# Weighted sums of attention issued once per head instead of twice, with a reordered start and double conversion buffers, in a fused attention and MLP kernel

## The chip, the cores and the metric

The kernel runs on one core of one Trainium2 chip. The metric is the device time of one execution in microseconds, as the median of several runs. The engines are TensorE (PE, with its weight loads as PEld), VectorE (DVE), ScalarE (ACT), GpSimd (POOL) and SyncE (SP, which here only issues DMAs).

## What is computed

Inputs are `q`, `k`, `v` of 2 batches, 8 heads, 768 positions and 64 features. The reference, cut to what matters:

```python
q_bits = (np.einsum('bhsd,dk->bhsk', q, proj) > 0)     # 6 bits each
mask = q_bucket[:, :, :, None] == k_bucket[:, :, None, :]
scores = np.where(mask, scale * q @ k.T, -1e9)
attn = exp(scores - max); attn = attn / (sum + 1e-9)
x = (attn @ v) with heads side by side                 # [2, 768, 512]
h = relu(x @ w_in); u, v = halves of h
v_s = w_spatial @ layernorm(v) + b_spatial
x = (u * v_s) @ w_out                                  # the first MLP, "moe1"
out = x + relu(layernorm(x) * g_ln @ w_ch1) @ w_ch2    # the second MLP
```

The weights of the MLPs arrive as 64-bit floats.

## The kernel before, in words

**A planner sets the order.** The body doesn't issue instructions. Each call on `nc` goes to `Plan.add`, which makes a job of it, notes which earlier jobs it must follow, and gives it a cost from a table (`Plan.cost`). Consecutive PE calls of the same shape into the same PSUM tile become one job that isn't broken up: up to 6 calls, or 12 where an fp32 matmul is less than 256 columns wide. `settle` lays all jobs out over time several times, with a latest due time for each job, and `issue` writes out the best order it found, engine by engine. So the order of every engine's queue comes from these costs and due times, and a changed cost or job moves instructions far away as well. All instructions are issued from one line of `issue`, line 492; the profile's rows are therefore told apart by tile names.

**Parts.** Part 0 is the attention of both batches, with `moe1` of batch 0 mixed into the attention of batch 1. Part 1 is `moe1` of batch 1 together with the begin of the second MLP; part 2 is the rest of the second MLP. An engine finishes its jobs of a part before it takes those of the next.

**Attention.** It goes through 96 query tiles of 128 queries: for each batch, for each of 8 heads, two groups (`g`) of three tiles (`j`). `attn_step` handles one tile:

- `scores`: four PE matmuls fill `sc` (128 x 768, two PSUM buffers of pool `ps_s`) from `qs` and `ks`. For each of two column ranges, one pass takes all 128 rows and a second takes 76 rows, of which 12 are mask rows, which make the score of a masked-out pair very large.
- `masked_max`: DVE reads `sc`, writes `x` to SBUF and its row extremes `nb`.
- `exps`: ACT takes exponentials of `x` in place, and sums them.
- `transposes`: six PE transposes turn `x` through PSUM tiles `pt` (two of 384 columns, pool `ps_b`, four buffers); ACT or DVE copies each to `e`, the transposed exponentials of a whole group (128 x 6 x 384, `EB` = 2 buffers).
- `weighted`: after a group's last tile, the product with `v`. `vv` is the stationary operand, 128 x 64, and `e` the moving one. Each group makes 12 calls: for each of the six key tiles, the left half of PE's columns takes the first 192 queries of the group and the right half the other 192. The sums `po` are in PSUM, 64 partitions for each half, and ACT copies one half to `xT`, DVE the other. An fp32 matmul shows as two records in the trace, so a group has 24 records of 128 x 192.
- `summed` and `normalized`: for each pair of heads, the sums' reciprocals are made (`zr`, `zw`), transposed through `pz`, and multiplied into `xT`.

`passes_of` moves high parts, low parts and mask rows into `ks` and `qs` by DMA from SP's queue, for each head and each query group.

**The start.** For head pair 0 the raw `k` and `q` are loaded (`pair_load`), and rows 64 to 127 of head 0's operands come by a second load, `dup` (`first_load`, in a buffer of `e`). `mismatch` makes the mask: PE multiplies raw `k` and `q` with `sides` (the projection `pj` with its signs, 32 columns for each of four quarters) into `pm` of 128 x 384, and DVE turns that into `m`. `first_parts` makes the operands of head 0 directly, without DMAs: high parts, low parts (`ks`, `qs`) and copies of the mask rows from `m`. `pair_split` makes the high parts (ACT) and low parts (DVE) of the whole pair, from which DMAs fill the operands of the second query group and of head 1. Before and after stand some PE transposes without use of their result (`warm`).

**Conversions.** While attention runs, 12 pieces of the first MLP's weights are converted: a 512 KB load on ACT's DMA queue into `f64`, `words_f64` with one ACT and five DVE instructions that use a second tile `f64c`, `join_f64` on POOL, and a split into high and low parts on ACT and POOL. Pool `conv0` has `CB0` = 1 buffer for each of the two tiles.

The change touches `Plan.__init__`, `Plan.add` and `Plan.cost`, the constants `CB0` and `EB`, the loads of `pj`, `mismatch`, `weighted`, `attn_step` and the calls that open part 0.

Of the kernel before, what the change touches and what calls it, by code (L numbers as in the profile page):

```python
# [18 lines left out]
P = 128  # L19
# [150 lines left out]
class Plan:  # L170
# [14 lines left out]
    RATE = {"load": 300e3, "move": 195e3, "store": 200e3}  # L185

    def __init__(self, tc):
        self.tc, self.jobs, self.pools, self.part = tc, [], [], 0
        for name, key in (("tensor", "PE"), ("vector", "DVE"), ("scalar", "ACT"), ("gpsimd", "POOL"), ("sync", "SP")):
            setattr(self, name, Engine(self, key))  # L190

    def add(self, engine, op, args, kw):
        writes = [kw["out"] if "out" in kw else args[0]]
        rest = [*(args if "out" in kw else args[1:]), *(x for k, x in kw.items() if k not in ("out", "accum_out"))]
        if "accum_out" in kw:
            writes.append(kw["accum_out"])
        reads = [x for x in rest if isinstance(x, View)]
        views = [(x, True) for x in writes if isinstance(x, View)] + [(x, False) for x in reads]
        prev = self.jobs[-1] if self.jobs else None
        if (  # L200
            engine == "PE"
            and prev is not None
            and prev.engine == "PE"
            and prev.part == self.part
            and not prev.closed
            and prev.out is writes[0].base
            and prev.kind == (op, cells(writes[0]), writes[0].rows)
            and len(prev.calls) < (12 if cells(writes[0]) < 256 and op == "matmul" and reads[0].dtype == F32 else self.RUN)
        ):
            job = prev  # L210
        else:
            job = Job(len(self.jobs), engine, self.part)
            self.jobs.append(job)
            if engine == "PE":
                job.out, job.kind = writes[0].base, (op, cells(writes[0]), writes[0].rows)
        busy, lag = self.cost(engine, op, writes, [x for x in rest if hasattr(x, "dtype")], kw, job)
        job.calls.append((op, args, kw))
        job.busy, job.lag = job.busy + busy, lag
        for x, w in views:
            for j, box, w2 in x.base.uses:  # L220
                if (w or w2) and j is not job and all(a < d and c < b for (a, b), (c, d) in zip(box, x.place)):
                    job.after.add(j)
            x.base.uses.append((job, x.place, w))
        return None
# [5 lines left out]
    def cost(self, engine, op, writes, reads, kw, job):  # L230

        out = writes[0]
        n = cells(out)
        if op == "dma_start":
            src = kw["in_"]
            sbuf = lambda x: isinstance(x, View) and not x.base.ring.pool.dram
            job.way = "store" if not sbuf(out) else "move" if sbuf(src) else "load"
            job.bytes = 4 * n * (out.rows if isinstance(out, View) else src.rows if isinstance(src, View) else 128)
            if engine == "ACT":
                return 0.4, 0.0  # L240
            return (0.84 if n <= 512 and job.bytes < 32768 else 0.61 if job.bytes < 200000 else 0.45), 0.0
        psum = any(isinstance(x, View) and x.base.ring.pool.psum for x in (out, *reads))
        if engine == "PE":
            if op == "transpose":
                return (0.109 if isinstance(reads[0], View) else 0.213), 0.165
            if reads[0].dtype == F32:
                return n * (0.00083 if out.rows == 64 else 0.00042) + 0.006 + (0 if job.calls else 0.2), 0.2
            return n * 0.4375e-3 + 0.0065, 0.17
        if engine == "ACT":
            if "accum_out" in kw:  # L250
                return 0.93, 0.1
            return 0.05 + n * 0.9e-3, 0.1
        if engine == "DVE":
            one = len([x for x in reads if cells(x) > 8]) < 2
            if op == "bn_stats":
                return 0.59, 0.1
            if n < 32:
                job.shared = not psum and op == "tensor_scalar"
                return 0.08, 0.11
            fast = op == "tensor_scalar" and one and not psum and "accum_out" not in kw  # L260
            job.shared = not psum and op in ("tensor_scalar", "scalar_tensor_tensor")
            held = sum(1 for x in reads if cells(x) == 1)
            return 0.065 + n * (0.53e-3 if fast else 1.04e-3) + 0.06 * held, 0.085
        if op == "memset":
            return 0.145, 0.05
        if kw.get("op") == ALU.pow:
            return 0.45 + 0.25 * n, 0.05
        return (0.06 + n * 2.42e-3 if op == "tensor_tensor" else 0.19 + n * 0.84e-3), 0.03
# [229 lines left out]
def attn_moe_kernel(ctx: ExitStack, tc: tile.TileContext, qT, kT, v, proj, w_in, w_spT, b_sp, w_out, g_ln, w1, w2, out):  # L498
# [14 lines left out]
    NKT = S // P  # L513
    GRP = 3
    TB = 4
    CB0 = 1
    VB = (((0, 1, 2), (3, 4, 5)), ((0, 1), (2, 3, 4), (5,)))
    CB = 2
    CONV_AT = (5, 9, 14, 19, 24, 29, 34, 39, 44, 49, 53, 57)
# [11 lines left out]
    AT = (-10, -7, -6, -4, 0)  # L531
    PO = 2
    KCUT = (0, 2)
    EB = 2
    GW = GRP * P
    NG = NQT // GRP
    KC = S // 2
# [57 lines left out]
    NM = 2 * NB  # L595
    MR = D + NM
    pj = const.tile([P, NB], F32, name="pj")
    for a in range(2):
        nc.scalar.dma_start(out=pj[a * D : (a + 1) * D], in_=proj)


    HROW = 3 * NB
# [95 lines left out]
    def mismatch(b, r):  # L698
# [9 lines left out]
            )  # L708
        nc.vector.tensor_scalar(m, pm, above, worth, op0=ALU.is_gt, op1=ALU.mult)
        pairs[b, r]["m"] = m  # L710

    order = [(b, h, g, j) for b in range(B) for h in range(H) for g in range(NG) for j in range(GRP)]
    NT = len(order)
# [119 lines left out]
            else:  # L833
                nc.vector.tensor_copy(e, pt)

    def weighted(b, h, g):
        gm = f"{b}_{h}_{g}"
        gr = groups[b, h, g]
        po = ps_b.tile([P, 512], F32, tag="b", name=f"po_{gm}")

        HW = GW // 2
        for kt in range(NKT):
            for a in range(2):
                nc.tensor.matmul(
                    po[a * D : (a + 1) * D, :HW],
                    heads[b, h]["vv"][:, kt],
                    gr["e"][:, kt, a * HW : (a + 1) * HW],
                    start=(kt == 0),
                    stop=(kt == NKT - 1),
                )  # L850
        groups.pop((b, h, g))
        own = slice(h % 2 * D, (h % 2 + 1) * D)
        at = g * GW
        nc.scalar.activation(xT[b][own, h // 2, at : at + HW], po[0:D, :HW], AF.Copy)
        nc.vector.tensor_copy(xT[b][own, h // 2, at + HW : at + GW], po[D:P, :HW])

    def summed(b, r):

# [18 lines left out]
    def attn_step(i):  # L877
# [9 lines left out]
        if 0 <= i + 1 < NT:  # L887
            masked_max(*order[i + 1])
            exps(*order[i + 1])
        if 0 <= i - PO < NT and order[i - PO][3] == GRP - 1:  # L890
            weighted(*order[i - PO][:3])
        for late, e in ((1, summed), (3, normalized)):
            n = i - PO - late
            if 0 <= n < NT and order[n][1] % 2 == 1 and order[n][2:] == (NG - 1, GRP - 1):
# [241 lines left out]
            nc.tensor.transpose(warm, ident, ident)  # L1136
    pair_load(0, 0, first=True)
    dup = first_load()
    mismatch(0, 0)
    first_parts(dup)  # L1140
    pair_split(0, 0, first=True)
    for _ in range(WARM2):
        nc.tensor.transpose(warm, ident, ident)
    head_prep3(0, 0)
# [220 lines left out]
```

## Time and profile before

| | us |
|---|---|
| runs: median of 3 | 674.24 |
| runs: lowest and highest | 673.82, 676.37 |
| profiled execution, device time | 673.77 |
| profiled execution, span of its instructions | 671.5 |
| PE covered by matmul records | 656.8 (98%) |
| PEld | 535.3 (80%) |
| DVE | 436.6 (65%) |
| ACT | 304.7 (45%) |
| POOL | 195.9 (29%) |

The times of rows are microseconds from the start of the span, which is 2.3 us shorter than the execution's device time. An engine's busy time is the union of its records. The end of a matmul record is modelled, and matmuls overlap, so PE's steps are read from the starts of records, not from their lengths. "Idle before" in a row is the time in which the engine had nothing to do just before, with the engine or DMA that ended it.

### The profile page before, as it was taken

The numbers are of one execution on the slowest core, as the hardware profiler recorded it, in microseconds if no ns is written. First come the engines' busy times: TensorE is split into PE (matmuls) and PEld (weight loads), VectorE is DVE, ScalarE is ACT, GpSimd is POOL, SyncE is SP. The second block draws the span as 40 slices with busy tenths as digits, with TensorE's granted clock in tenths as the row PEclk, the third lists the DMA queues.
The fourth block names the chain that finished last, engine by engine and source line by source line (L and its number), as shares of the span: only waits on it lengthen the run. The fifth ranks groups of instructions, "written<-read, shape, count | busy, mean of one in ns | idle before, by whom it ended". The sixth has DMA issues, their size and how long they took to land.

```text
span 671.5 us, 10197 instructions
## 1 busy us (share of the span) xinstructions
PE 656.8 (98%) x3760; PEld 535.3 (80%) x3760; DVE 436.6 (65%) x820; ACT 304.7 (45%) x597; POOL 195.9 (29%) x184
## 2 busy tenths in 40 slices
PE   7999999999999999999999999999999999999997
PEld 6887777877788788887778888888888888888886
DVE  5889778897666554444699697766893258962122
ACT  4887777876565644443364344432331122321110
POOL 2333324344341431110224424134442014540000
PEclk7999999999999999999999999999999999999999
DMA  6676766747536824452652441632220022310031
GB/s 180 163 180 164 199 155 145 195 114 190 187 68 210 246 64 131 159 193 95 227 179 91 146 143 62 215 118 86 85 94 1 15 79 86 102 33 0 1 126 62
DMA packets 47417, 83.78 MB, mean 125 GB/s; under 512 B 5676, under 2 KB 32136, under 8 KB 46344
## 3 DMA queue, kind: packets, MB, share of 16 engines
q1 hardware_dynamic: 34024, 53.64, 28.5%
q10 hardware_dynamic: 13344, 29.50, 13.6%
q8 instruction: 30, 0.49, 0.3%
q14 instruction: 19, 0.16, 0.1%
HBM read 51.42 MB, written 12.58 MB: 95 GB/s over the span
## 4 chain that ended last, share of the span: by engine, by line
PE 77%; DVE 9%; DMA 7%; ACT 3%; issue 3%; POOL 1%; SPq 1%; ACTq 0%; DVEq 0%; POOLq 0%
PE pc L492 20%; PE acc L492 20%; PE pg L492 8%; PE sc L492 6%; PE po L492 6%; PE pv L492 5%; PE pt L492 5%; PE py L492 4%; DMA f_v<-in_w_in 3%; DVE x L492 2%; DMA f_w<-in_w 1%; ACT x L492 1%; DVE f64c_v L492 1%; PE ptr_g L492 1%; DMA f_u<-in_w_in 1%
## 5 line engine op out<-in xcount | busy, mean ns | idle before, releaser
L492 PE MATMUL pc<-xh,w1t 128*128 128x512 f32 x576 | 142.0, 394 | 0.0
L492 PE MATMUL acc<-w2t,ch 128*128 128x512 f32 x576 | 141.2, 393 | 0.0
L492 PEld LDWEIGHTS acc<-w2t,ch 128*128 128x128 f32 x576 | 108.1, 188 | 24.6
L492 PEld LDWEIGHTS pc<-xh,w1t 128*128 128x128 f32 x576 | 108.0, 188 | 24.6
L492 ACT ACTIVATE x<-x,nb 128x768 f32<-128x768 f32 x96 | 89.7, 935 | 36.6 <-DVE x L492 32.9
L492 DVE TENSOR_SCALAR_CACHE_REDUCE x<-sc 128x768 f32<-128x768 f32 x96 | 90.7, 953 | 20.3 <-PE sc L492 11.9
L492 PE MATMUL sc<-ks,qs 128*128 128x512 f32 (+3 forms) x384 | 94.4, 368 | 6.2 <-DVE qs L492 3.3
L492 DVE SCALAR_TENSOR_TENSOR ch<-pc,ch 128x512 fp32r<-128x512 f32 x48 | 33.0, 687 | 87.9 <-ACT ch L492 87.7
L492 ACT ACTIVATE ch<-pc 128x512 fp32r<-128x512 f32 x48 | 28.6, 596 | 127.3 <-PE pc L492 127.0
L492 PE MATMUL pt<-ident,x 128*128 128x128 f32 x576 | 82.4, 276 | 1.3 <-ACT x L492 0.6
L492 PEld LDWEIGHTS sc<-ks,qs 128*128 128x128 f32 (+1 forms) x384 | 64.8, 194 | 21.4 <-issue 7.2
L492 POOL TENSOR_TENSOR f64c_w<-f_w,f64c_w 128x512 f32<-128x512 f32 x32 | 44.7, 1398 | 123.3 <-DVE f64c_w L492 108.0
L492 PEld LDWEIGHTS pt<-ident,x 128*128 128x128 f32 x576 | 66.7, 141 | 13.3 <-ACT x L492 3.3
L492 PE MATMUL po<-e,vv 128*64 128x192 f32 x768 | 69.5, 330 | 1.1 <-DVE xT L492 1.0
L492 ACT ACTIVATE e<-pt 128x384 f32<-128x384 f32 x120 | 55.5, 485 | 31.8 <-PE pt L492 31.1
L492 PEld LDWEIGHTS po<-e,vv 128*64 128x64 f32 x768 | 52.4, 137 | 12.5 <-issue 2.4
L492 DVE COPY e<-pt 128x384 f32<-128x384 f32 x72 | 39.6, 553 | 21.6 <-PE pt L492 21.0
L492 DVE TENSOR_SCALAR f64c_w<-f64c_w 128x512 f32<-128x512 f32 (+1 forms) x64 | 38.7, 607 | 19.1 <-ACT f64c_w L492 18.3
L492 PE MATMUL pg<-vn,w_sp 128*128 128x512 f32 x180 | 45.1, 400 | 0.0
L492 ACT ACTIVATE f64c_w<-f_w 128x512 f32<-128x512 f32 x32 | 21.4, 669 | 46.5 <-DMA f_w<-in_w 43.9
L492 PEld LDWEIGHTS pg<-vn,w_sp 128*128 128x128 f32 x180 | 33.0, 188 | 7.8 <-issue 0.6
L492 PE MATMUL pv<-w_v,act_x 128*128 128x512 f32 x144 | 36.4, 398 | 0.6 <-DVE act_x L492 0.6
(132 smaller groups left out, 790.7 us busy)
## 6 DMA issues: line engine op xcount, KB each, us to landing
f_w<-in_w ACTq DMA_DIRECT2D x32, 512.0 KB
ks<-k SPq DMA_DIRECT2D x45, 192.0 KB
qs<-q SPq DMA_DIRECT2D x31, 192.0 KB
wst_sp<-in_w_spT SPq DMA_DIRECT2D x12, 384.0 KB
w_out<-ws_out SPq DMA_DIRECT2D x2, 2048.0 KB
vv<-in_v SPq DMA_DIRECT2D x16, 192.0 KB
ot<-y_dram SPq DMA_DIRECT2D x12, 256.0 KB
qs<-q SPq DMA_DIRECT2D x31, 96.0 KB
```

Source lines behind the costliest of these rows:

```text
L492: getattr(getattr(nc, engine[j.engine]), op)(*map(live, args), **{k: live(x) for k, x in kw.items()})
```

## The change

- `weighted` is called once per head, after both of its groups. There are again 12 calls, but the left half of PE's columns takes all 384 queries of group 0, the right half those of group 1. The copies to `xT` are one of 384 columns on ACT and one on DVE per head.
- `e` has three buffers instead of two.
- The planner keeps the 12 calls of 384 fp32 columns as one job, and counts 0.27 us instead of 0.2 for the first call of an fp32 job.
- Everything that `pair_split` of the first pair issues, high parts and low parts, now waits for the mask `m` (`plan.behind`).
- One of the two loads of `pj` is issued by SP instead of ACT.
- `conv0` has two buffers each of `f64` and `f64c`.

```diff
--- before.py
+++ after.py
@@ -185,7 +185,7 @@
     RATE = {"load": 300e3, "move": 195e3, "store": 200e3}
 
     def __init__(self, tc):
-        self.tc, self.jobs, self.pools, self.part = tc, [], [], 0
+        self.tc, self.jobs, self.pools, self.part, self.behind = tc, [], [], 0, None
         for name, key in (("tensor", "PE"), ("vector", "DVE"), ("scalar", "ACT"), ("gpsimd", "POOL"), ("sync", "SP")):
             setattr(self, name, Engine(self, key))
 
@@ -205,7 +205,7 @@
             and not prev.closed
             and prev.out is writes[0].base
             and prev.kind == (op, cells(writes[0]), writes[0].rows)
-            and len(prev.calls) < (12 if cells(writes[0]) < 256 and op == "matmul" and reads[0].dtype == F32 else self.RUN)
+            and len(prev.calls) < (12 if cells(writes[0]) == 384 and op == "matmul" and reads[0].dtype == F32 else self.RUN)
         ):
             job = prev
         else:
@@ -213,6 +213,8 @@
             self.jobs.append(job)
             if engine == "PE":
                 job.out, job.kind = writes[0].base, (op, cells(writes[0]), writes[0].rows)
+        if self.behind:
+            job.after.add(self.behind)
         busy, lag = self.cost(engine, op, writes, [x for x in rest if hasattr(x, "dtype")], kw, job)
         job.calls.append((op, args, kw))
         job.busy, job.lag = job.busy + busy, lag
@@ -244,7 +246,7 @@
             if op == "transpose":
                 return (0.109 if isinstance(reads[0], View) else 0.213), 0.165
             if reads[0].dtype == F32:
-                return n * (0.00083 if out.rows == 64 else 0.00042) + 0.006 + (0 if job.calls else 0.2), 0.2
+                return n * (0.00083 if out.rows == 64 else 0.00042) + 0.006 + (0 if job.calls else 0.27), 0.2
             return n * 0.4375e-3 + 0.0065, 0.17
         if engine == "ACT":
             if "accum_out" in kw:
@@ -513,7 +515,7 @@
     NKT = S // P
     GRP = 3
     TB = 4
-    CB0 = 1
+    CB0 = 2
     VB = (((0, 1, 2), (3, 4, 5)), ((0, 1), (2, 3, 4), (5,)))
     CB = 2
     CONV_AT = (5, 9, 14, 19, 24, 29, 34, 39, 44, 49, 53, 57)
@@ -531,7 +533,7 @@
     AT = (-10, -7, -6, -4, 0)
     PO = 2
     KCUT = (0, 2)
-    EB = 2
+    EB = 3
     GW = GRP * P
     NG = NQT // GRP
     KC = S // 2
@@ -595,8 +597,8 @@
     NM = 2 * NB
     MR = D + NM
     pj = const.tile([P, NB], F32, name="pj")
-    for a in range(2):
-        nc.scalar.dma_start(out=pj[a * D : (a + 1) * D], in_=proj)
+    nc.sync.dma_start(out=pj[0:D], in_=proj)
+    nc.scalar.dma_start(out=pj[D:P], in_=proj)
 
 
     HROW = 3 * NB
@@ -708,6 +710,7 @@
             )
         nc.vector.tensor_scalar(m, pm, above, worth, op0=ALU.is_gt, op1=ALU.mult)
         pairs[b, r]["m"] = m
+        return plan.jobs[-1]
 
     order = [(b, h, g, j) for b in range(B) for h in range(H) for g in range(NG) for j in range(GRP)]
     NT = len(order)
@@ -833,26 +836,22 @@
             else:
                 nc.vector.tensor_copy(e, pt)
 
-    def weighted(b, h, g):
-        gm = f"{b}_{h}_{g}"
-        gr = groups[b, h, g]
-        po = ps_b.tile([P, 512], F32, tag="b", name=f"po_{gm}")
-
-        HW = GW // 2
+    def weighted(b, h):
+        po = ps_b.tile([P, GW], F32, tag="b", name=f"po_{b}_{h}")
         for kt in range(NKT):
-            for a in range(2):
+            for g in range(NG):
                 nc.tensor.matmul(
-                    po[a * D : (a + 1) * D, :HW],
+                    po[g * D : (g + 1) * D],
                     heads[b, h]["vv"][:, kt],
-                    gr["e"][:, kt, a * HW : (a + 1) * HW],
+                    groups[b, h, g]["e"][:, kt],
                     start=(kt == 0),
                     stop=(kt == NKT - 1),
                 )
-        groups.pop((b, h, g))
         own = slice(h % 2 * D, (h % 2 + 1) * D)
-        at = g * GW
-        nc.scalar.activation(xT[b][own, h // 2, at : at + HW], po[0:D, :HW], AF.Copy)
-        nc.vector.tensor_copy(xT[b][own, h // 2, at + HW : at + GW], po[D:P, :HW])
+        nc.scalar.activation(xT[b][own, h // 2, 0:GW], po[0:D], AF.Copy)
+        nc.vector.tensor_copy(xT[b][own, h // 2, GW:S], po[D:P])
+        for g in range(NG):
+            groups.pop((b, h, g))
 
     def summed(b, r):
 
@@ -887,8 +886,8 @@
         if 0 <= i + 1 < NT:
             masked_max(*order[i + 1])
             exps(*order[i + 1])
-        if 0 <= i - PO < NT and order[i - PO][3] == GRP - 1:
-            weighted(*order[i - PO][:3])
+        if 0 <= i - PO < NT and order[i - PO][2:] == (NG - 1, GRP - 1):
+            weighted(*order[i - PO][:2])
         for late, e in ((1, summed), (3, normalized)):
             n = i - PO - late
             if 0 <= n < NT and order[n][1] % 2 == 1 and order[n][2:] == (NG - 1, GRP - 1):
@@ -1136,9 +1135,11 @@
             nc.tensor.transpose(warm, ident, ident)
     pair_load(0, 0, first=True)
     dup = first_load()
-    mismatch(0, 0)
+    made = mismatch(0, 0)
     first_parts(dup)
+    plan.behind = made
     pair_split(0, 0, first=True)
+    plan.behind = None
     for _ in range(WARM2):
         nc.tensor.transpose(warm, ident, ident)
     head_prep3(0, 0)
```

## Rows read from the trace of the kernel before

**Rows 1.** Windows: span, length, busy us of PE, PEld, DVE, ACT, POOL, clock, DMA.

```profile
24.00:136.00 112.00, 109.36 (x904) 88.54 (x902) 95.14 (x200) 88.02 (x196) 43.41 (x41) 1.00 0.68 169
150.00:317.00 167.00, 165.07 (x1095) 135.61 (x1096) 93.28 (x201) 86.15 (x176) 45.78 (x42) 1.00 0.51 152
317.00:671.00 354.00, 349.88 (x1551) 284.23 (x1549) 220.67 (x365) 105.77 (x179) 96.24 (x70) 1.00 0.29 94
```

**Rows 2.** Waits of PE in the whole run: us in total, times, longest.

```profile
PE sc L492 <- DVE qs L492: 3.3, 1, 3.3
PE sc L492 <- DMA qs<-q: 0.8, 1, 0.8
PE sc L492 <- DVE f64c_out L492: 0.6, 1, 0.6
```

**Rows 3.** Timeline of PE around the first block, short windows: start, length.

```profile
22.36 0.82 PE L492 MATMUL pt<-ident,x 128*128 128x128 f32 x6
...
23.11 0.55 PE L492 MATMUL po<-e,vv 128*64 128x192 f32 x4
...
24.78 0.49 PE L492 MATMUL po<-e,vv 128*64 128x192 f32 x4
25.21 0.33 PE L492 MATMUL pt<-ident,x 128*128 128x128 f32 x1
```

**Rows 4.** Timeline of PE around one mask.

```profile
26.01 0.52 PE L492 MATMUL pm<-k,sides 128*32 128x384 f32 x2
...
26.36 0.49 PE L492 MATMUL pm<-k,sides 128*32 128x384 f32 x2
```

**Rows 5.** Groups of the whole run: count, busy us, mean ns, idle before.

```profile
L492 PEld LDWEIGHTS po<-e,vv 128*64 128x64 f32 x768 | 52.4, 137 | 12.5 <-issue 2.4 <-DVE xT L492 1.2 <-ACT e L492 1.2
L492 ACT ACTIVATE xT<-po 64x192 f32<-64x192 f32 x32 | 10.2, 320 | 10.1 <-PE po L492 7.8 <-DVE xT L492 2.0
L492 DVE COPY xT<-po 64x192 f32<-64x192 f32 x32 | 11.5, 359 | 23.8 <-ACT xT L492 18.8 <-PE po L492 4.5
L492 ACT ACTIVATE e<-pt 128x384 f32<-128x384 f32 x120 | 55.5, 485 | 31.8 <-PE pt L492 31.1
L492 DVE COPY e<-pt 128x384 f32<-128x384 f32 x72 | 39.6, 553 | 21.6 <-PE pt L492 21.0
```

**Rows 6.** Timeline of the start, all engines: start, length.

```profile
5.83 0.32 DVE L492 TENSOR_SCALAR sides<-pj 64x6 f32<-64x6 f32 x3 [1.35 <-DMA pj<-in_proj]
...
6.88 0.95 POOL L492 TENSOR_SCALAR ks<-dup 64x768 fp32r<-64x768 f32 x1 [3.44 <-DMA dup<-in_kT]
...
6.99 0.49 PE L492 MATMUL pm<-q_raw,sides 128*32 128x384 f32 x2
7.05 1.58 DVE L492 SCALAR_TENSOR_TENSOR k<-k_raw,k 128x768 fp32r<-128x768 f32 x1
8.56 0.94 DVE L492 SCALAR_TENSOR_TENSOR q<-q_raw,q 128x768 fp32r<-128x768 f32 x1
...
9.42 0.66 DVE L492 TENSOR_SCALAR m<-pm,above,worth 128x384 fp32r<-128x384 f32 x1
...
10.42 0.88 SPq L492 DMA_DIRECT2D qs<-m  x1
...
10.82 4.64 PE L492 MATMUL sc<-ks,qs 128*128 128x512 f32 x12 [3.33 <-DVE qs L492]
...
16.39 1.09 PE L492 MATMUL sc<-ks,qs 128*128 128x512 f32 x4
```

**Rows 7.** Windows of the start, columns as in rows 1.

```profile
7.50:9.80 2.30, 0.00 (x0) 0.00 (x0) 2.30 (x3) 0.31 (x1) 0.33 (x1) 1.00 0.70 178
9.90:16.60 6.70, 5.78 (x19) 4.80 (x20) 4.34 (x10) 3.01 (x7) 1.10 (x2) 0.50 0.61 165
16.70:20.00 3.30, 3.30 (x25) 2.97 (x24) 2.49 (x5) 2.80 (x7) 0.46 (x1) 1.00 0.82 253
```

**Rows 8.** Groups from 24 to 136 us: count, busy us, mean ns.

```profile
L492 DVE TENSOR_SCALAR_CACHE_REDUCE x<-sc 128x768 f32<-128x768 f32 x47 | 44.3, 950 | 7.3 <-PE pt L492 3.0 <-PE sc L492 2.9 <-ACT e L492 0.9
```

## The prediction

> **What bounds the kernel now.** I read the windows first, to see which engine fills which stretch. TensorE (PE) is covered for 349.88 of 354 us after the attention and for 165.07 of 167 us in the second batch, so there the end is set by PE's own work [rows 1]. In the first batch, 24 to 136 us, PE is covered for 109.36 of 112 us, but VectorE (DVE) is busy for 95.14 us and ScalarE (ACT) for 88.02: two engines run close behind it. Next the waits of PE, which are few: the longest, 3.3 us, is at the very start, a scores matmul that waits for DVE's `qs` [rows 2]. So a microsecond taken out of PE's queue, or off its start, is a microsecond of the end, provided that DVE and ACT keep up in the first batch. The parts are costed in that order.
>
> **Part 1, the weighted sums.** Today 32 blocks of 24 PE records each. One is seen in [rows 3]: it starts at 23.11, and the next instruction starts at 25.21, so a block holds PE for 2.10 us. The records come in pairs, one for each column half. In the last four records (0.49 us, one record lasting 0.33) the second pair starts 0.16 us after the first; in the first four (0.55 us) it starts 0.22 after. The last pair starts at 24.94 and the next instruction at 25.21, 0.27 later. So the block is 0.22, ten steps of 0.162, and 0.26: twelve steps of 0.162 and some 0.16 us that every block pays at its two ends. The entry costs more: the last of six transposes starts at 22.91 (five steps of 0.11 after 22.36), and the block 0.20 after it, where another transpose would start after 0.11: 0.09.
>
> After the change there are 16 blocks, again of 24 records, each over 384 columns. Twice the step is 0.324; twelve of them and 0.16 are 4.05 us. Per head: two blocks with two entries, 4.38, against 4.05 and 0.09, 4.14: 0.24 less, times 16 heads **3.8 us** off PE. No row shows this matmul. The nearest with 384 columns is the mask's, whose second pass starts 0.35 us after its first, at 26.01 and 26.36 [rows 4]. Twelve steps of that plus the 0.10 at the exit are 4.30, 4.39 with the entry, and nothing is gained; that is the lower bound. If the 0.002 over 0.16 belongs to a record and not to a column, and the end cost shrinks to 0.10, it is 0.32 a step, 3.94 a block, 5.6 us in all: the upper bound. I stay near the doubled step, because the 0.35 is the first step of its block, and first steps are longer here too (0.22 against 0.16).
>
> A block covers the load of its weights today: a weight load lasts 137 ns [rows 5] and a pair has two of them, yet a pair takes 0.162 us. The Trainium skill, "TensorE: Matmul & The Clock Gate", under "The mechanism" of packing, says that loads overlap running matmuls only where the row group differs, and the two halves here have the same rows. By that rule the loads would be exposed and halving them would give far more; the step of 0.162 us speaks against it.
>
> The copies out of PSUM also halve in number: ACT 32 of 320 ns become 16 of about 485 (its copy of 384 columns), DVE 32 of 359 become 16 of about 553 [rows 5]. That is 10.2 to 7.8 us and 11.5 to 8.8 us. I count nothing for it: both lie beside PE. It helps part 4.
>
> **Part 2, the start.** The mask's matmuls end at 7.48, but DVE makes the mask `m` only at 9.42, since it does the low parts of `k` (7.05, 1.58 us) and of `q` (8.56, 0.94 us) first [rows 6]. After `m` come the low part of `qs` and the mask rows' copies, and 1.4 us after the start of `m` the first scores, at 10.82. Put straight behind the matmuls, `m` starts near 7.55: 1.9 us earlier, and the scores near 8.9. Next late would be POOL's copy of `dup`, done at 7.83, which is early enough. What moves behind: DVE's 2.52 us, and the two high parts on ACT, which has little to do before the first exponentials (3.01 of 6.7 us from 9.9 to 16.6). What now waits for `m` on ACT and DVE has behind it in their queues the first exponentials and maxima, which need scores that need `m` themselves, so no one is held up who could run; POOL has no part in it. DVE's 2.52 us must fit in the gaps between the first row maxima: in those 6.7 us DVE is busy for 4.34 [rows 7], so most fits; I charge 0.4. Their DMAs move too: `qs<-m`, the last of SP's transfers for query group 1, was issued at 10.42, and the first tile to use it has its scores at 16.39. Two microseconds later for it and two earlier for the scores leave some 2 us; SP issues it behind the low part of `q`, and behind it stand the transfers for head 1, needed much later. One `proj` load goes from ACT's queue to SP's: DVE waited for the second until 5.83, the last 1.35 us of it idle, so `sides` can come sooner; but if SP takes it first, the raw loads each shift by one issue (0.88 us for `qs<-m`). I count these as zero, plus or minus 0.9. Net **1.5 us** gained; bounds: 1.5 lost (all 2.52 and the 0.9 come back against 1.9) and 3.3 gained (the whole wait).
>
> **Part 3, the second conversion buffer.** PE's only wait on a conversion is 0.6 us (`f64c_out`), and its only wait on a DMA is 0.8 [rows 2]. Larger reach for the 512 KB loads could take the first away or lengthen the second. Zero, between 0.6 gained and 0.8 lost.
>
> **Part 4, the coarser block.** Sixteen blocks of 2.10 us fill PE in the first batch; the rest of its 109.36 us is 75.8 for 47 tiles, 1.61 us a tile. DVE needs 95.14 / 47 = 2.02 a tile [rows 1, 8]. So between blocks DVE is the slower one, and it catches up while PE is in a block. Two score buffers let it do two maxima of 0.95 us: 1.9, nearly a block of today. In a block of 4.05 it has 2.15 us beyond them, for which it needs other work: a copy of `e` (0.55), one of `xT`, or a conversion's words. Where it finds only the copy of `e`, it idles 1.6 us a head. Its slack is (112 - 95.14) / 8, 2.1 us a head, so most is absorbed; I charge 0.2 a head for eight heads, 1.6. The second batch, with DVE at 93.28 of 167 us, pays nothing. Bounds: 0.5 gained by the shorter copies, 12.8 lost (8 x 1.6).
>
> **The sum** for this execution (span 671.5, time 673.77; the median of the runs, 674.24, is 0.47 above it): -3.8 - 1.5 + 0 + 1.6 = -3.7, so 670.1; for a median I say 670.2.
>
> **Rivals.**
> A, the start goes better than costed. The granted clock was still 1.00 up to 9.8 us and 0.50 (1.2 GHz) from 9.9 to 16.6, after PE had stood idle from 7.5 to 10.8 [rows 7]. If scores from 8.9 on keep it up, the first three tiles take 1.09 us each, as the four records at 16.39 do, and not 4.64 / 3 = 1.55 [rows 6]: 1.4 us more. With 0.7, half of the 1.35, from `proj` coming early: 668.0. Against it, ACT was the busiest engine right after, 2.80 of 3.30 us at full clock.
> B, slower: DVE runs dry in the long block and PE waits for it between blocks. Place: the first batch, every head; price: 1.6 us times 8, so 673.8 - 5.3 + 12.8 = 681.3. It decides when DVE's idle time in a block exceeds its slack, which needs DVE to have no conversion at hand there. For it: 85% busy. Against: conversions are spread over the batch.
> C, a block isn't cheaper (0.35 a step): 673.8 - 1.5 + 1.6 = 673.9, no change. For it, the only row with 384 columns; the change would then not do what it says.
> D, the low parts return in full at the start, 2.1 us more than charged, so the order gains nothing: 672.2.
> E, the loads are exposed as the page has it: half of 52.4 us of weight loads goes [rows 5], 673.8 - 26.2 = 647.6. The pair step speaks against it.
>
> **How the numbers follow.** Forecast 50 (40 of it below the bound), A 13, B 10, C 14, D 11, E 2. A measurement here tells about 0.5%, 3.4 us, from no change: faster below 670.9. Faster: 40 + 13 + 2 = 55; same: 10 + 14 + 11 = 35; slower: B, 10. The range leaves out B, E and the edges of A: 665.5 to 675.0.
>
> **What would show it.** Right: 384 `po` records of 128x384 in 16 blocks, each some 4.0 to 4.1 us from its first start to the next instruction, their busy total near 66 us against 69.5; first scores near 9 us with `m` before the low parts; PE's cover in the first batch still near 98%. Wrong: a block of 4.3 us (C), scores still after 10 us or a new wait on `qs` for the fourth tile (D), PE idle for over 1 us a head after a block with DVE `x` as releaser (B), or a clock that never falls at the start (A).

## The result, and the profile after

The changed kernel takes **669.14 us** (median of 7 runs, 665.71 to 672.32), the kernel before 674.24 (7 runs, 673.48 to 676.37): ratio 0.9912, interval 0.9884 to 0.994. It is faster by some 5 us; 670.2 was forecast. The profiled execution took 669.14, its span 666.8 us. In the changed kernel all instructions come from line 494.

The windows of the changed kernel answer to [rows 1], with the same columns:

```profile
24.00:136.00 112.00, 109.50 (x740) 78.21 (x742) 97.68 (x200) 89.94 (x196) 43.38 (x41) 1.00 0.71 184
150.00:317.00 167.00, 166.66 (x943) 127.47 (x942) 92.75 (x192) 83.81 (x167) 46.32 (x41) 1.00 0.51 162
317.00:667.00 350.00, 343.95 (x1521) 279.87 (x1519) 211.71 (x358) 103.53 (x173) 96.95 (x70) 1.00 0.26 87
```

PE is covered in the first batch as it was (109.50 of 112 us; cover alone doesn't tell how far PE got), with DVE busier (97.68 against 95.14). In the last stretch 6 us are uncovered, where 4.1 were before. PE's waits in the whole run (us in total, times, longest), which answer to [rows 2]:

```profile
PE sc L494 <- DVE x L494: 3.6, 3, 1.7
PE pv L494 <- ACT xT L494: 2.2, 1, 2.2
PE sc L494 <- DVE qs L494: 1.8, 2, 1.5
...
PE sc L494 <- DMA qs<-m: 0.7, 1, 0.7
```

The wait on `qs` at the start shrank from 3.3 to 1.5 us at most. Longer are the waits of scores on the row maxima (`x`; before there was one, of 0.5 us), the longest at the start, and new is one of 2.2 us on ACT's copy `xT`, in the first MLP of batch 1.

**A block.** PE's timeline around the first block (start, length), short windows as in [rows 3]:

```profile
27.56 0.27 PE L494 MATMUL pt<-ident,x 128*128 128x128 f32 x1
27.76 0.87 PE L494 MATMUL po<-e,vv 128*64 128x384 f32 x4
...
31.04 0.81 PE L494 MATMUL po<-e,vv 128*64 128x384 f32 x4
31.36 0.49 PE L494 MATMUL po<-e,vv 128*64 128x384 f32 x2
31.78 0.50 PE L494 MATMUL sc<-ks,qs 128*128 128x512 f32 x1
```

The block starts at 27.76 and the next instruction at 31.78: 4.02 us. Pairs follow each other after 0.32 (31.04, 31.36), the last pair holds PE for 0.42, and the entry after a transpose takes 0.20 as before. All 16 blocks measure 4.02. Their groups (count, busy us, mean ns, idle before), against [rows 5]:

```profile
L494 PE MATMUL po<-e,vv 128*64 128x384 f32 x384 | 65.5, 490 | 0.0
L494 DVE COPY xT<-po 64x384 f32<-64x384 f32 x16 | 9.0, 560 | 29.3 <-ACT xT L494 24.7 <-PE po L494 4.5
L494 ACT ACTIVATE xT<-po 64x384 f32<-64x384 f32 x16 | 7.7, 484 | 23.1 <-PE po L494 22.5 <-DVE xT L494 0.4
```

**The start**, timeline of DVE and PE, against [rows 6]:

```profile
7.55 0.68 DVE L494 TENSOR_SCALAR m<-pm,above,worth 128x384 fp32r<-128x384 f32 x1 [1.94 <-PE pm L494]
...
8.96 0.47 PE L494 MATMUL sc<-ks,qs 128*128 128x512 f32 x1 [1.52 <-DVE qs L494]
...
9.60 1.47 DVE L494 SCALAR_TENSOR_TENSOR q<-q_raw,q 128x768 fp32r<-128x768 f32 x1
...
10.99 0.95 DVE L494 SCALAR_TENSOR_TENSOR k<-k_raw,k 128x768 fp32r<-128x768 f32 x1
11.86 0.94 DVE L494 TENSOR_SCALAR_CACHE_REDUCE x<-sc 128x768 f32<-128x768 f32 x1
...
12.86 1.65 PE L494 MATMUL sc<-ks,qs 128*128 128x512 f32 x4 [1.74 <-DVE x L494]
```

The mask comes at 7.55 and the first scores at 8.96. But `q`'s and `k`'s low parts now stand between the first scores and their maximum, which starts at 11.86; before, it started at 12.79:

```profile
12.79 0.96 DVE L492 TENSOR_SCALAR_CACHE_REDUCE x<-sc 128x768 f32<-128x768 f32 x1 [1.37 <-PE sc L492]
```

Of 1.9 us, 0.9 is left at that point, and nothing at the sixth maximum, which starts at 20.84 (before at 20.53). The windows of the start, columns as above:

```profile
9.00:12.00 3.00, 1.85 (x8) 1.23 (x8) 2.96 (x5) 1.14 (x2) 1.04 (x1) 1.00 0.24 51
12.00:16.00 4.00, 3.14 (x11) 2.88 (x12) 2.82 (x7) 2.78 (x6) 0.00 (x0) 0.51 0.94 203
16.00:20.00 4.00, 4.00 (x20) 3.65 (x19) 1.88 (x4) 2.74 (x7) 0.00 (x0) 0.64 0.81 219
```

DVE is full from 9 to 12 (2.96 of 3 us), and the granted clock still falls to its lower level, only later than in [rows 7]. It also rises later, at about 18.9 us (an estimate from the mean of 0.64, as 0.50 up to there and 1.00 after), where it was up again by 16.7; part of what was lost up to the sixth maximum may be that.

**Where 2 us went back.** PE began the first MLP of batch 1, the begin of part 1, at 317.10 before and at 310.41 after. These are the first matmuls behind that border, the kernel before first:

```profile
317.10 0.70 PE L492 MATMUL pv<-w_v,act_x 128*128 128x512 f32 x2
...
310.41 0.73 PE L494 MATMUL pv<-w_v,act_x 128*128 128x512 f32 x2
```

PE was 6.7 us ahead there; at the end of the span 4.7 were left. The timeline of the changed kernel behind the border, where ACT loads and converts pieces of the second MLP's weights:

```profile
325.03 1.90 POOL L494 TENSOR_TENSOR f64c_w<-f_w,f64c_w 128x512 f32<-128x512 f32 x1 [3.80 <-DVE f64c_w L494]
...
326.95 0.39 ACTq L494 DMA_DIRECT2D f_w<-in_w  x1
...
327.44 0.60 ACT L494 ACTIVATE xT<-pv 128x512 f32<-128x512 f32 x1 [4.00 <-POOL f64c_w L494]
...
328.09 1.75 PE L494 MATMUL pv<-w_u,act_x 128*128 128x512 f32 x6 [2.18 <-ACT xT L494]
```

ACT issues the third load of these pieces at 326.95, just after POOL has joined the first piece and so freed a buffer. The copy `xT` stands behind that issue in ACT's order and starts after 4.00 us of idle time, and PE waits 2.18 us for it. Then the clock falls:

```profile
325.00:330.00 5.00, 2.82 (x11) 1.95 (x11) 4.82 (x11) 2.37 (x4) 4.14 (x3) 0.95 0.33 106
330.00:334.00 4.00, 4.00 (x13) 3.15 (x12) 2.06 (x5) 1.56 (x3) 0.51 (x1) 0.64 0.00 1
```

At a mean granted clock of 0.64 for 4 us, PE does 2.6 us of full-clock work, so the spell costs about 1.4 us more by this estimate.

### The profile page after: what moved, and what is told of

The parts are those of the page before. It is cut to its first block, busy times and chain, and to the rows that moved or that the text cites. A ratio compares the mean times of both kernels' runs of the same rounds, so it can differ in the third digit from the quotient of the medians.

```text
span 666.8 us, 9374 instructions
## 1 busy us (share of the span) xinstructions
PE 651.5 (98%) x3376; PEld 510.2 (77%) x3376; DVE 430.3 (65%) x804; ACT 302.1 (45%) x581; POOL 198.3 (30%) x184
## 4 chain that ended last, share of the span: by engine, by line
PE 87%; DVE 7%; DMA 3%; issue 1%; ACT 1%; POOL 0%; SPq 0%; ACTq 0%; DVEq 0%; POOLq 0%
PE pc L494 20%; PE acc L494 20%; PE pv L494 8%; PE po L494 8%; PE sc L494 8%; PE pg L494 8%; PE pt L494 7%; PE py L494 5%; DVE x L494 2%; DMA f_w<-in_w 1%; DVE f64c_u L494 1%; PE pm L494 1%; PE ptr_g L494 1%; PE px_c L494 1%; DMA qs<-m 1%
## 5 line engine op out<-in xcount | busy, mean ns | idle before, releaser
L494 PE MATMUL po<-e,vv 128*64 128x384 f32 x384 | 65.5, 490 | 0.0
L494 PEld LDWEIGHTS po<-e,vv 128*64 128x64 f32 x384 | 26.2, 137 | 31.3 <-issue 30.1
L494 PE MATMUL pv<-w_u,act_x 128*128 128x512 f32 x144 | 36.3, 400 | 2.3 <-ACT xT L494 2.2
L494 DVE TENSOR_SCALAR f64c_w<-f64c_w 128x512 f32<-128x512 f32 x64 | 32.6, 511 | 7.2 <-ACT f64c_w L494 6.5
```

Source lines behind the costliest of these rows:

```text
L494: getattr(getattr(nc, engine[j.engine]), op)(*map(live, args), **{k: live(x) for k, x in kw.items()})
```

## The experiments

Runs of one set share a chip and the runs of the kernel before. Times are medians.

| set | kernel | us (lowest to highest) | ratio to before (interval) |
|---|---|---|---|
| 1 | sums_only | 669.25 (668.41 to 671.18) | 0.9920 (0.9899 to 0.9942) |
| 1 | start_only | 673.99 (671.53 to 675.60) | 0.9991 (0.9977 to 1.0005) |
| 1 | buffers_only | 669.47 (669.07 to 671.18) | 0.9925 (0.9904 to 0.9946) |
| 1 | split_columns | 665.82 (664.85 to 667.25) | 0.9867 (0.9847 to 0.9888) |
| 2 | after_again | 668.80 (665.60 to 670.77) | 0.9923 (0.9899 to 0.9946) |
| 2 | cost_only | 672.59 (670.73 to 677.12) | 0.9986 (0.9965 to 1.0006) |
| 2 | buffers_same_order | 671.05 (670.33 to 673.74) | 0.9964 (0.9951 to 0.9977) |
| 2 | late_load | 665.41 (664.62 to 666.38) | 0.9881 (0.9857 to 0.9904) |
| 3 | old_start | 663.74 (662.84 to 666.54) | 0.9843 (0.9819 to 0.9867) |
| 3 | late_low | 665.07 (663.30 to 668.74) | 0.9862 (0.9833 to 0.9891) |
| 3 | fill_start | 665.31 (663.47 to 666.69) | 0.9853 (0.9829 to 0.9877) |
| 3 | late_low_fill | 664.11 (662.59 to 670.02) | 0.9848 (0.9817 to 0.9879) |

The kernel before: 674.43, 674.24 and 674.31 in the three sets.

### Each part alone: sums_only, start_only, buffers_only

Each is the kernel before with one part of the change; the planner then makes a new order. sums_only has `weighted` per head, the third buffer of `e`, the job of 12 calls and the cost of 0.27:

```diff
-    EB = 2
+    EB = 3
...
-    def weighted(b, h, g):
+    def weighted(b, h):
...
```

> The kernel before with the weighted sums once per head and the third buffer of e alone; the start and the conversion buffers stay. Theory: what the change gives is the fixed cost at the ends of 16 blocks that are gone. So 16 blocks of 4.02 us, PE records of po covering 65.5 us against 69.5, and 668.5 to 671.5 us, 3 to 5 below before. Rival (the start or the buffers carry the gain): 672.5 to 675 us.

Measured 669.25: 5.2 us faster, and `po` is busy for 65.5 us as in the changed kernel. start_only has the mask first and one load of `pj` on SP:

```diff
+    nc.sync.dma_start(out=pj[0:D], in_=proj)
...
+    plan.behind = made
     pair_split(0, 0, first=True)
+    plan.behind = None
```

> The kernel before with the new start alone (mask ahead of the low parts, one load of proj on the sync queue). Theory: first scores near 9.0 us and not 10.8, but the two low parts then stand ahead of the first row maximum, so the third tile's scores wait for DVE and most of the 1.9 us is given back: 672.5 to 674.5 us. Rival (the start carries the gain): 669 to 671.5 us.

Measured 673.99, an interval that holds no change. buffers_only:

```diff
-    CB0 = 1
+    CB0 = 2
```

> The kernel before with two conversion buffers alone. Theory: no term of the sum, 672.5 to 675.5 us. Rival (the buffers relieve DVE and ACT in the first batch, where PE's steps lose most): 669 to 671.5 us, with less idle time of PE between 24 and 150 us.

Measured 669.47, 5.0 us faster: the theory's time is missed, the rival's is met. That a part costed at zero gives as much as the weighted sums was the surprise, and as each kernel was planned anew, two causes were open: the buffer itself, or a luckier order.

The three times can't be read as the worth of the parts, since each new order also meets the border in its own way. The first matmuls behind the border, in sums_only, start_only and buffers_only, and then PE's longest wait behind it in the last two:

```profile
312.64 0.73 PE L492 MATMUL pv<-w_v,act_x 128*128 128x512 f32 x2
...
311.84 0.71 PE L494 MATMUL pv<-w_v,act_x 128*128 128x512 f32 x2
...
310.29 0.48 PE L492 MATMUL pv<-w_v,act_x 128*128 128x512 f32 x1
...
328.96 1.20 PE L494 MATMUL pv<-w_v,act_x 128*128 128x512 f32 x4 [2.25 <-DVE act_x L494]
...
326.46 1.19 PE L492 MATMUL pv<-w_v,act_x 128*128 128x512 f32 x4 [1.59 <-DVE act_x L492]
```

Against 317.10 they are 4.5, 5.3 and 6.8 us ahead at the border; by the spans, 5.0, 0.5 and 3.8 are left at the end. start_only and buffers_only lose 4.7 and 3.0 us behind the border, with PE waiting and the granted clock at means of 0.53 and 0.76 from 330 to 334 us. So the 0.4 us of start_only doesn't measure the start.

### The buffer or the order: cost_only, buffers_same_order

cost_only changes only a figure of the planner, so that the order alone changes:

```diff
-                return ... + (0 if job.calls else 0.2), 0.2
+                return ... + (0 if job.calls else 0.27), 0.2
```

> The kernel before with only the planner's cost of an fp32 job's first call raised from 0.2 to 0.27 us: the same work in another order. Theory (the plan of before happens to lose 12 to 13 us of PE's steps between 24 and 150 us, and any new plan loses less there): 668.5 to 672 us, with the loss of that stretch at 9 us or less. Rival (each part alone saved its own work, and the gains overlap): 673 to 676 us, the stretch unchanged.

Measured 672.59, interval 0.9965 to 1.0006, single runs from 670.73 to 677.12: not to be told from no change, and a miss for the theory's numbers. It does show how widely another order's runs scatter. Its profiled execution, the longest of the ten, began the first MLP of batch 1 at 316.95, level with before, so this new order brought nothing up to there.

buffers_same_order keeps the order that the planner made for one buffer, and gives the pool two:

```diff
-... = self.pool.real.tile(..., bufs=self.bufs)
+... = self.pool.real.tile(..., bufs=2 if self.pool.name == "conv0" else self.bufs)
```

> The kernel before, its order of all queues kept as planned for one conversion buffer, but with two real buffers under it. Theory (the new order brought the 5 us of the run with two buffers, not the memory): 673 to 675.5 us. Rival (a conversion's load or first step waits for its buffer and holds ACT or DVE): 669 to 671.5 us.

Measured 671.05, 3.2 us faster with the same order of instructions: the theory is missed, and the buffer itself pays. Three pairs of lines show where. First ACT's queue, PE and a window of 2 us (columns as above, the last two the DMA share and GB/s) in the kernel before, then the same with two buffers, the window 0.93 us earlier, as this execution leads by that much already:

```profile
28.55 0.34 ACTq L492 DMA_DIRECT2D f_out<-in_w_out  x1
...
35.36 0.71 PE L492 MATMUL sc<-ks,qs 128*128 128x512 f32 x2 [0.58 <-DVE f64c_out L492]
...
29.00:31.00 2.00, 2.00 (x26) 1.63 (x24) 2.00 (x4) 1.25 (x2) 2.00 (x2) 1.00 0.70 89
```

```profile
27.05 0.33 ACTq L492 DMA_DIRECT2D f_out<-in_w_out  x1
...
33.69 0.70 PE L492 MATMUL sc<-ks,qs 128*128 128x512 f32 x2
...
28.07:30.07 2.00, 2.00 (x26) 1.63 (x24) 2.00 (x6) 0.88 (x2) 2.00 (x2) 1.00 0.80 263
```

With one buffer the load is issued after POOL's join of the piece before; with two it is 1.5 us earlier, 0.93 of which is the lead. The scores at 35.36 lose their wait of 0.58. The profile names DVE's `f64c_out` for that wait, as the last thing done before it. But in PE's queue the stop is at the step that waits for two transfers into `ks` and `qs`. Their records end by 34.59 with one buffer and by 32.88 with two, 1.71 us earlier; the load's own packets end at 32.17 and 30.34. DVE and ACT, on the other hand, start their maxima and exponentials in between 0.93 to 0.98 us earlier, which is no more than the lead. So the load that comes sooner is out of the way of the transfers that PE needs, and PE gains 0.74 us. That the load slowed these transfers is read from the times; no run tests it by itself.

Instruction by instruction the lead goes from 0.93 at 30 us to 1.67 behind these scores and in smaller steps up and down to 2.56 at 155 us, where the last step of 0.46 again stands at scores that waited for a transfer (ended at 154.17 and 151.68). After that it stays nearly level, at 2.4 in the end. The 0.93 arose in the first 25 us, where in that one profile the spell at the lower clock was shorter, which the buffer doesn't explain. So 1.6 of the 3.2 us is shown in this profile; the rest isn't. At the border this kernel is 2.5 us ahead and buffers_only 6.8: the other 4.3 came with the new order.

### Ends or loads of a block: split_columns

The changed kernel in its own order, with each 384-column call issued as two of 192: as many records and weight loads as before, but in 16 blocks.

```diff
+for a in range(2):
+    part_of = slice(a * 192, a * 192 + 192)
+    for op, args, kw in j.calls:
+        nc.tensor.matmul(live(args[0][:, part_of]), live(args[1]), live(args[2][:, part_of]), **kw)
```

> The changed kernel in the same order, but each weighted-sum matmul of 384 columns issued as two of 192, the first columns of all key tiles and then the second: one block of 48 records per head. Theory (the ends of a block are what costs): the block goes from 4.02 to 4.07 us, 24 steps of 0.162 and 0.16, and the time rises by 0.8 us at most, 668.5 to 670.5. Rival (the number of matmuls and weight loads costs): a block of 4.2 us or more, and the 4 us saved are lost again, 672.5 to 674.5 us.

A block takes 4.05 us (27.46 to 31.52 for the first), 0.03 more than with half the records. The first block and the groups of that kernel:

```profile
27.46 4.12 PE L498 MATMUL po<-e,vv 128*64 128x192 f32 x48
31.52 0.50 PE L501 MATMUL sc<-ks,qs 128*128 128x512 f32 x1
...
L498 PE MATMUL po<-e,vv 128*64 128x192 f32 x768 | 65.9, 328 | 0.0
L498 PEld LDWEIGHTS po<-e,vv 128*64 128x64 f32 x768 | 53.8, 137 | 9.3 <-issue 1.2 <-ACT x L501 0.3 <-DVE ve_v L501 0.2
```

Twice the loads (53.8 us against 26.2 of loading) cost 16 × 0.03, half a microsecond. So the gain of the sums comes from the ends of the blocks, of which 16 are gone, and not from fewer records. The whole kernel ran at 665.82, below the 668.5 expected and below the changed kernel's 669.14 and 668.80 of other sets; the split doesn't explain that. In its profile ACT's copy at the border is also 3.5 us late, but the clock stays at 1.00 after it, so part of it may be that the spell there comes in some executions and not in others. The records of the single runs fit that: of the changed kernel's thirteen runs the two shortest, 665.60 and 665.71, have mean granted clocks of 0.995 and 0.994, as the four of split_columns have (0.994 to 0.995); the other eleven have 0.989 to 0.994.

### The border: after_again, late_load

after_again is the changed kernel, unaltered, beside its variant.

> The changed kernel itself, as the reference of this set: 668 to 670 us.

late_load moves the issue of the third load behind the copy `xT` and the split of the activations in ACT's order; nothing else moves:

```diff
+        job_of("ACT", "f64_w1_1").start = job_of("ACT", "act_x1_4").start + 0.001
         order = sorted(...)
```

> The changed kernel with one instruction moved in ACT's queue: the third load of second-MLP weights stands behind the next copy of pv and the next split of x instead of ahead of them. Theory (ACT stands 4.0 us at this load, which waits for its buffer, and PE waits 2.2 us for the copy behind it, after which the granted clock is 0.5 for 3.4 us): the wait of PE on xT near 325 us is gone and the time falls by 2 to 4 us against the changed kernel of this set. Rival (PE would then wait for the next thing, the conversion itself): less than 1 us.

Measured 665.41 against 668.80, 3.4 us less (the two intervals overlap a little). The timeline of late_load at the same place:

```profile
323.75 0.60 ACT L502 ACTIVATE xT<-pv 128x512 f32<-128x512 f32 x1 [1.23 <-PE pv L502]
...
324.94 1.55 PE L502 MATMUL pv<-w_u,act_x 128*128 128x512 f32 x6
...
325.98 0.39 ACTq L502 DMA_DIRECT2D f_w<-in_w  x1
```

```profile
325.00:330.00 5.00, 5.00 (x23) 4.00 (x22) 4.82 (x10) 2.41 (x4) 3.67 (x3) 1.00 0.32 107
330.00:334.00 4.00, 4.00 (x21) 2.99 (x20) 4.00 (x11) 4.00 (x8) 0.00 (x0) 1.00 0.01 4
```

The copy goes ahead as soon as PE has made its input, the load is issued when POOL's join is done, as before, and PE doesn't stop; the clock stays at 1.00. Against after_again's profile, the longest of its six runs, PE gains 5.1 us between 318 and 337 us, 4.3 of which last to the end; against the first profile of the changed kernel 3.2 last. The medians differ by 3.4, as the clock's spell is part of it and differs between executions. The four runs of late_load lie below all but two of the changed kernel's thirteen. As split_columns shows, an execution without the spell comes near this time with the load unmoved, so the 3.4 us is not the wait alone.

### The start: old_start, late_low, fill_start, late_low_fill

All four change late_load at the start alone. old_start puts the low and high parts of the first pair ahead of the mask again:

```diff
+        put(job_of("ACT", "k2_0_0"), first + 0.001)
+        put(job_of("ACT", "q2_0_0"), first + 0.002)
+        put(job_of("DVE", "k2_0_0"), second + 0.001)
+        put(job_of("DVE", "q2_0_0"), second + 0.002)
```

> The kernel with the late load (665.4 us), every queue in the same order but for the start: the high and low parts of the first pair stand ahead of the mask again, as before the change. Theory (the order of the start gains little, since the row maxima wait behind the low parts instead): first scores near 10.8 us, but the instructions after 30 us come at most 1.0 us later than with the late load alone; 665 to 666.5 us. Rival (the 1.9 us at the first scores stay): they come 1.5 to 2 us later, 667 to 667.5 us.

Measured 663.74 against late_load's 665.41 of another set: not slower, and below both forecasts. The timeline of DVE and PE:

```profile
5.54 0.94 DVE L514 SCALAR_TENSOR_TENSOR k<-k_raw,k 128x768 fp32r<-128x768 f32 x1
...
7.35 0.96 DVE L514 SCALAR_TENSOR_TENSOR q<-q_raw,q 128x768 fp32r<-128x768 f32 x1 [0.87 <-ACT q L514]
8.23 0.67 DVE L514 TENSOR_SCALAR m<-pm,above,worth 128x384 fp32r<-128x384 f32 x1
...
9.63 0.47 PE L514 MATMUL sc<-ks,qs 128*128 128x512 f32 x1 [2.20 <-DVE qs L514]
...
12.05 0.96 DVE L514 TENSOR_SCALAR_CACHE_REDUCE x<-sc 128x768 f32<-128x768 f32 x1 [1.29 <-PE sc L514]
```

DVE stood idle for 1.94 us ahead of the mask in the changed kernel, waiting for `pm`. Here the low parts fill most of that time, so the first scores come at 9.63 and not at the 10.8 expected, and the first maximum at 12.05. With the mask first, scores come sooner, but the first maximum comes no sooner: at 11.86 in the changed kernel, 12.00 in after_again, 12.47 in late_load, three executions of one start. So putting the mask first moved work out of idle time and into the path, and gained nothing at the maximum. What does help both orders is a part of the change that old_start keeps, the load of `pj` on SP's queue: `sides` is done at 4.7 us, and was done at 6.15 before, so `k`'s low part starts at 5.54 and not at 7.05.

late_low keeps the mask first and moves `k`'s low part behind the second maximum:

```diff
+        put(job_of("DVE", "k2_0_0"), job_of("DVE", "x_0_0_0_1").start + 0.001)
```

> The kernel with the late load, and the low part of k of the first pair made behind the second row maximum instead of ahead of the first. Theory (the low parts hold the maxima): the first maximum starts near 11.1 instead of 11.9 us, PE's wait for it shrinks from 1.7 to about 1 us, and what follows comes 0.5 to 0.9 us earlier; 664.5 to 665 us. Rival (it is only held elsewhere, by the transfers of head 1's keys or later maxima): no shift after 30 us.

The first maximum starts 1.2 us sooner (11.29 against 12.47), 0.65 of which is there at the mask already (7.42 against 8.07), ahead of anything that was moved; 665.07 shows no clear gain. fill_start puts 12 and 10 transposes without use of their result where PE is idle, after the mask's matmuls and after the second tile's scores; late_low_fill does both, with 12 and 8:

```diff
+        fill = {job_of("PE", "pm_0_0"): 12, late: 10}
...
+                for _ in range(fill.pop(j, 0)):
+                    nc.tensor.transpose(live(self.warm[0]), self.warm[1], self.warm[1])
```

> The kernel with the late load, with 12 transposes of the identity more behind the first mask's matmuls and 10 behind the second tile's scores, where PE stands idle (their result is not used). Theory (PE's idle time there lets the granted clock fall to 0.5 for 3.4 to 6.8 us, and the tiles in it take 1.6 us each instead of 1.0): the clock stays at 1.00 from 7 to 20 us, and the instructions after 30 us come 1 to 2.5 us earlier; 663 to 664.5 us. Rival (DVE and ACT pace the start whatever PE's clock): under 0.5 us.

> Both of the last two together, with 12 and 8 transposes. Theory: both shifts add up to 1.5 to 3 us, 662.5 to 664 us. Rival: no more than the better of the two.

The windows of fill_start:

```profile
12.00:16.00 4.00, 3.30 (x24) 2.69 (x22) 3.57 (x8) 3.17 (x8) 0.00 (x0) 1.00 0.96 207
16.00:20.00 4.00, 3.26 (x24) 2.86 (x23) 2.98 (x7) 4.00 (x11) 0.00 (x0) 1.00 0.73 171
```

The clock stays at 1.00, yet PE now stands idle for 0.7 us in each 4, and ACT is full from 16 to 20: at full clock another engine sets the pace there. The first weighted block starts at 26.2 us, in late_low_fill at 24.4, against 27.5 in late_load. Medians of 665.31 and 664.11 don't tell either from late_load or old_start by their intervals. In the profiled executions the leads do last: compared with late_load at the same instruction, fill_start is 1.3 us ahead at 25 us and 1.2 at the end, late_low_fill 3.3 and 2.7 (with one spell at the low clock near 146 us), late_low 1.8 and 1.8, old_start 0.2 and 1.0. Each is a single execution, and late_load's came late to its mask (8.07 us; the changed kernel's 7.55 with the same start), so these leads may be too large; the medians don't confirm them.

## Why the prediction was right, point by point

The time was right, 669.1 for 670.2, and so was the main term. Of the other three each was off, what they missed cancelled, and a loss at the border that no term had took 2 us back: that the sum came within 1.1 us was luck.

**Part 1 (3.8 us, bounds 0 to 5.6): right.** The step was 0.323 for 0.324, the block 4.02 for 4.05, the entry unchanged; per head 4.38 became 4.11, 0.27 × 16 = 4.3 us. The estimate by the doubled step held, and rival C, built on the mask's 0.35, fell: a first step of a block is longer (here 0.37), as the prediction argued. sums_only gives 5.2, of which a new order may hold a part. In the second batch, where PE alone sets the pace, its lead over before, by the start of a head's last `po` record, grows from 2.92 us in the fourth head to 4.32 in the eighth, a steady 0.35 a head; what the 0.08 over 0.27 is, isn't shown. Rival E fell twice: blocks halved in load count aren't cheaper than their ends explain, and split_columns, with the loads doubled again, adds 0.03 us a block. The rule of the Trainium skill, "TensorE: Matmul & The Clock Gate", "The mechanism" of packing, that loads overlap only where the row group differs, doesn't describe these blocks: 137 ns loads, two to a pair, hide in a pair of 0.162 us as in one of 0.323. The same section also lets a load run ahead into a background weight buffer; no run here tells whether that is what happens.

**Part 2 (1.5 us, bounds -1.5 to 3.3): the gain wasn't there, within the bounds.** Mask at 7.55 and scores at 8.96 were right to 0.1 us. The step that failed is the charge of 0.4 for DVE's 2.52 us: the gaps in which they were to fit lay behind the first maximum, but both low parts ran ahead of it. Until the sixth maximum the whole 1.9 us was lost again, as rival D has it. start_only shows 0.4 us with an interval that holds none, but lost 4.7 at the border and so doesn't settle it; old_start, in one order, does better: with the mask first nothing is gained at the first maximum. What the prediction counted as nothing, `sides` coming sooner, made the old order better too: `k`'s low part can then run before the mask's matmuls are done.

**Part 3 (0, bounds -0.8 to 0.6): wrong.** buffers_same_order gives 3.2 us. The failed step is reading a buffer's worth from the waits of PE that name the conversion (0.6). The profile names the engine that was updated last, and the wait of 0.6 was for transfers that landed later, by the times because the load was still moving. At 154.69 the same kind of wait stands under another name (`e`). About 1.6 us is followed in the trace; 0.9 more is the clock at the start of that one execution, and the rest of the 3.2 stays open.

**Part 4 (-1.6 us): not seen.** PE's cover in the first batch is 109.50 for 109.36, the last block of that batch ends some 3 us earlier than before, both in the changed kernel and in sums_only, and DVE, with 97.68 us busy, used its slack. Rival B, which needed PE idle after each block, fell: the waits on `x` come three times, 3.6 us, one of them 1.7 at the start. No sign of the charge of 0.2 a head is left.

**Rival A** fell: scores came early, and the clock fell all the same, to 0.51 from 12 to 16. fill_start holds it up; its profile ends 1.2 us ahead of late_load's, but the median shows no 1.4 us for it.

**What no step had:** the new order at the border, some 3.4 us by late_load, the clock's spell included. Without it the parts would have given about 8.8 us and the forecast would have been too small. The single parts add up to 10.6 us at the end, but start_only and buffers_only carry losses at the border too. Up to the border they add up to 16.5 us, and the changed kernel has 6.7 there. So some 10 us of the single gains don't add up. Whether each new order removes the same waits of the first batch, or was a lucky one, isn't shown.

## What to carry to other kernels

A block of column-tiled matmuls pays at its ends, so make blocks longer rather than merge their records. Don't cost a buffer by the waits that name it on the bounding engine: ask which transfers move at the same time as the load and which compute stands behind it on the issuing queue, and after any new plan look at the borders between stages for a DMA issue that holds up its engine's compute. Before moving work behind a critical step, see whether it was filling idle time ahead of it. Where every variant is planned anew, compare the kernels at the same instruction ahead of each border before calling a time the worth of a part.

## What was unexpected of the hardware

- Doubling the records and weight loads of a block at the same columns cost 0.03 us a block (4.05 against 4.02), while each block removed gave back about 0.27 us.
- An issue of a load on ACT's queue that waited for its buffer kept ACT's next activation from starting: 4.00 us idle, for some 2.9 of which that activation's own input was ready (in late_load it ran 2.2 us ahead of the same issue, and 3.7 us earlier, with PE 0.8 us ahead).
- Transposes added in PE's idle time, and nothing else added, kept the granted clock at 1.00 from 12 to 20 us, where late_load had 0.50 and 0.79 and the changed kernel 0.51 and 0.64 without them; and a PE pause of 2.2 us at 326 us was followed by a mean of 0.64 in the changed kernel's profile, but by 1.00 in that of split_columns after a pause of the same length.
